# Normalizations moved to VectorE, a reordered prologue list, and the first block's query products one pair a step

## The chip, the cores and the metric

The kernel runs on one core of a Trainium2 chip. The metric is the device time of one execution in microseconds; the time before the change is the median of three runs.

## The reference

All tensors are float32 and B = 1, S = 2048, D = 512, H = 32 heads of 16, F = 1792. One key and one value head serve all 32 query heads.

```python
mod = (silu(c) @ w_mod)                       # six rows of 512: sa, ca, ga, sb, cb, gb
h = layernorm(x) * (1 + ca) + sa
q, k, v = h @ wq, h @ wk, h @ wv              # q: 32 heads; k, v: one head each
p = softmax(q k^T / 4)                        # 32 x 2048 x 2048
x = x + ga * ((p v) @ wo)
h = layernorm(x) * (1 + cb) + sb
x = x + gb * ((sigmoid(h @ w_gate) * (h @ w_up)) @ w_down)
```

## The kernel before, in words

Matrix products with weights run as three float16 products (high by high, high by low, low by high), so most activations exist as a high and a low half. The sequence is cut into four blocks b of 512 rows, and each block's 32 heads into eight units of four heads: 32 units of 16 key tiles, 512 steps in the main loop (line 969). A step computes for one unit and one tile of 128 keys four score products (`st_tile`, tile st, a PSUM bank each), four exponentials on ACT (P <- st), and the products with V and the ones column (tile c) of the step two before it. Softmax subtracts a row maximum that is found ahead: `a_product` (line 515) multiplies queries by keys into a bank sa and `a_max` (526) reduces it on DVE (mx <- sa). Four maxima are taken in each step, and `A0 = 76` of them (line 55) before step 0, so the maxima run 19 steps ahead. When a unit's 64 maxima are there, `max_end` and `max_rows` (538, 545) reduce them, transpose them on PE and write them by DMA (mh) into rows of the unit's query tile qp: the score product then has the maximum already subtracted. So a score product of a unit waits for that DMA.

The **prologue** is everything before step 0. Its order is written out by hand in the string `PLAN` (36), each token of which names a function through `stages` (861) and its arguments: `S` statistics of one x tile, `ra`, `rb`, `rc` the inverse root (DVE, POOL, DVE), `N` the normalization of a tile of 128 rows (`ln_norm`, 386), `T` four transposes on PE into a bank pt, `H`, `E`, `L` the high half (ACT), the float32 copy (ACT or DVE) and the low half (POOL or DVE) of the modulated activation, `pk`, `KB`, `KL` the key product and its evictions into kp, `pv`, `V` the value product, `q`, `QA`, `QL` a query product of 128 columns, its eviction on ACT and its low half on POOL, `pm`, `me`, `pr`, `m` the modulation, `wh`, `wl` a piece of wq into halves, `a` a maxima product, `x` the maximum on DVE, `mx` a quarter of unit 0's maxima rows, and `lw`, `lx`, `lm` loads. All engines keep this order, except for loads and some POOL work that a scheduler places. Which engine does a piece is set by tables: `NORM` (51) sends the four normalizations of block 0 to DVE and the twelve others to POOL.

A finished query group is written to DRAM (qD, line 474) and read back rearranged as qp (500): the first maxima product of a query piece waits for both DMAs. All loads and these writes are issued by SP to one DMA queue. Blocks' query groups that the prologue leaves out, ten of sixteen, run in the first block in five couples: `Couple.part` (161) issues for each term two matmuls that use one half of PE's rows each, called a pair here, 24 pairs a couple. `light` (960) hands them out to the steps, beginning at step 2: 17 steps a couple, with one or two pairs a step by the table `ats`. After the last pair both groups of the couple are evicted at once by `end` (456): ACT writes the float32 copy q32, POOL makes high and low half, SP writes qD. `defer(n, f)` (662) has f called at the start of the step n later.

After the first block the feed-forward work of the block before takes the place of `light`, and the last block's stands after the loop.

Of the kernel before, what the change touches and what calls it, by code (L numbers as in the profile page):

```python
# [10 lines left out]
AF = mybir.ActivationFunctionType  # L11
ALU = mybir.AluOpType
# [6 lines left out]
D = 512  # L19
# [10 lines left out]
SH = 4.0  # L30
SW = 16.0
# [3 lines left out]

PLAN = (
# [12 lines left out]
)  # L49

NORM = ('DDDD', 'PPPP', 'PPPP', 'PPPP')
H32 = ('ADAD', 'AAAA', 'AAAA', 'AAAA')
HLO = ('PDPD', 'PPPP', 'PPPP', 'PPPP')

A0 = 76
LAG = 2


# [9 lines left out]
QSKIP = 2  # L68
# [11 lines left out]
def adaln_mqa_glu_kernel(  # L80
# [15 lines left out]
    pool, sp = nc.gpsimd, nc.sync  # L96
# [3 lines left out]
    x = x[0]  # L100
# [30 lines left out]
    pinned, first = [True], [True]  # L131
    pe, dve, act = Ordered(nc.tensor), Ordered(nc.vector), Ordered(nc.scalar)
    pool1 = Ordered(nc.gpsimd)
# [45 lines left out]
    def t32(name, shape=(P, 512)):  # L179
        return wp.tile(list(shape), F32, tag="f32", name=name, bufs=18)  # L180
# [176 lines left out]
    def xs(b):  # L357
        return [xall[:, 4 * b + t, :] for t in range(4)]
# [26 lines left out]

    def ln_norm(b, t):
        mv, ve, rs, nw = lns[b]
        eng = dve if NORM[b][t] == 'D' else pool1
        eng.tensor_scalar(xs(b)[t], xs(b)[t], mv[:, t, 0:1], rs[:, t:t + 1], op0=ALU.subtract, op1=ALU.mult)

    def ln1_tr(b, k):
        pts[b, k] = pt = bank("pt")
# [21 lines left out]
    def passes(ah, al, bh, bl):  # L414
        return ((ah, bh), (ah, bl), (al, bh))
# [34 lines left out]
    def q_group(b, o):  # L450
        def term(n, rs):
            k, i = divmod(n, 3)
            w_, h_ = passes(wqh[k], wql[k], h1[b][0][k], h1[b][1][k])[i]
            return w_[rs, o * P:(o + 1) * P], h_[rs]

        def end(pq, second):
            qdone.add((b, o))
            q2 = wp.tile([P, 2, 512], F16, tag="q2", name="q2", bufs=2)
            q32 = t32("q32")
            act.activation(q32, pq, AF.Identity, scale=1.0 / (SH * SW))  # L460
            if first:
                act.activation(q2[:, 0], pq, AF.Identity, scale=1.0 / (SH * SW))
                q2s[b, o] = q2, q32
                return
            pool.tensor_scalar(q2[:, 0], q32, 1.0, 0.0, op0=ALU.mult, op1=ALU.add)
            q_low(b, o, q2, q32)

        return Group("q", 12, "pq", term, end)

    q2s = {}  # L470

    def q_low(b, o, q2, q32):
        (pool1 if first else pool).tensor_tensor(q2[:, 1], q32, q2[:, 0], op=ALU.subtract)
        sp.dma_start(qD[:, o * P:(o + 1) * P, b * QB:(b + 1) * QB].rearrange("h p q -> p h q"), q2)
# [63 lines left out]
    def max_end(i, t0, t1):  # L538
        nt = t1 - t0
        n = 4 * nt  # L540
        m16 = wp.tile([P, n], F32, tag="m16", name="m16", bufs=4)
        dve.tensor_reduce(m16.rearrange("p (h t) -> p h t", t=nt), mxs[i][:, :, t0:t1, :], axis=AX.X, op=ALU.max)
        return lambda: max_rows(i, t0, t1, m16)
# [118 lines left out]
    def defer(n, f_):  # L662
        waits.append((now[0] + n, f_))
# [35 lines left out]
    class Transposes:  # L699
        stage, n = "tr", 4  # L700
# [145 lines left out]
    def q_part(b, o, k):  # L846
        if k == 0:
            groups[b, o] = q_group(b, o)
        g = groups[b, o]
        if k == 0:  # L850
            g.open()
        for n in range(3 * k, 3 * k + 3):
            pe.matmul(g.bank, *g.term(n, slice(0, P)), start=(n == 0), stop=(n == g.n - 1))

    def q_end(b, o):
# [3 lines left out]
    blanks.append(blank(pool1))  # L859

    stages = {"S": ln_stats, "ra": ln_eps, "rb": ln_pow, "rc": ln_newton, "N": ln_norm, "T": ln1_tr, "H": ln1_high,
              "E": ln1_full, "L": ln1_low, "pk": k_product, "KB": k_high, "KL": k_end, "pv": v_product, "V": v_end,
              "wh": wq_high, "wl": wq_low, "q": q_part, "QA": q_end, "QL": lambda b, o: q_low(b, o, *q2s.pop((b, o))),
# [3 lines left out]
    for tok in PLAN.split():  # L867
        name = tok.rstrip("0123456789")
        stages[name](*[int(z) for z in tok[len(name):]])
    assert not held and apos == A0  # L870
    first.clear()
# [18 lines left out]
    nw, wdone = len(wjobs), 0  # L890
    qleft = [(b, o) for b in range(NB) for o in range(4) if (b, o) not in qdone]
    early = [Couple(q_group(*z), q_group(*y)) for z, y in zip(qleft[::2], qleft[1::2])]
    main, spare = [], []
    run = []
# [63 lines left out]


    def light(s):  # L960
        c_, n = divmod(s - QSKIP, 17)
        if s >= QSKIP and c_ < len(early):
            ats = [0, *(12 * (k + 1) // 9 for k in range(9)), *(12 + 12 * (k + 1) // 8 for k in range(8))]
            early[c_].part(ats[n], ats[n + 1])

    vq = []
    before = None
# [1 line left out]
    for i, (b, u) in enumerate(units):  # L969
# [4 lines left out]
        for kb in range(NKB):  # L974
            s = i * NKB + kb
# [5 lines left out]
            rows = [max_end(*z) for z in late]  # L981
            an = A0 + 4 * s

# [6 lines left out]
            if before == "run":  # L990
                piece()
            elif b == 0:
                light(s)
# [78 lines left out]
```

## Time and profile before

| | |
|---|---|
| median of 3 runs (1729.25 to 1729.74) | 1729.47 us |
| the profiled execution | 1729.32 us |
| its span | 1727.5 us |
| mean granted TensorE clock | 0.994 |
| PE busy | 1685.0 us (98%) |
| DVE busy | 1422.0 us (82%) |
| ACT busy | 1236.0 us (72%) |
| POOL busy | 635.2 us (37%) |
| first score matmul of step 0 | at 108.7 us |

Busy times overlap; matmuls are pipelined and their ends are modelled. In the answers, a row of instructions gives its start, its length, the engine, the line, what it writes and reads (out<-in), a count, and in brackets the idle time of its engine before it and what ended that. A row of waits gives the sum, the number and the longest. Nearly all prologue and loop instructions have line 129, that of the helper that keeps them in order, so the tiles' names tell them apart. PEclk is the clock granted to TensorE as a share of full speed. A row of the chain of waits gives start, length and what the chain ran through.

### The profile page before, as it was taken

Reading aid. Unit: us, or ns where it says so; the run is one execution under the profiler, and the core shown is the slowest. Engines: PE = TensorE matmul, PEld = TensorE weight load, DVE = VectorE, ACT = ScalarE, POOL = GpSimd, SP = SyncE. Lnnn points to the kernel's source line nnn. Section 1 sums busy time; section 2 is a strip of 40 time slices with the busy share of each in tenths; the row PEclk is TensorE's granted clock in tenths of the full one; section 3 lists DMA queues with packets and bytes.
Section 4 is the critical chain, followed back from the end, with each engine's and each line's share of the span. In section 5 each row is a group of like instructions: output and inputs, shape, how many; then the busy total and the mean of one; then the engine's idle time right before and its main releaser. Section 6 shows DMA issues by size and latency. Waiting matters only on the chain.

```text
span 1727.5 us, 34861 instructions
## 1 busy us (share of the span) xinstructions
PE 1685.0 (98%) x13971; PEld 571.6 (33%) x13971; DVE 1422.0 (82%) x2359; ACT 1236.0 (72%) x2253; POOL 635.2 (37%) x732
## 2 busy tenths in 40 slices
PE   5899999999999999999999999999999999999998
PEld 2323333322323333333333333333333333323443
DVE  7789999999998898988898988898898888941311
ACT  4358888888878777777778777777778777774100
POOL 6642444444254231332154232233254141231533
PEclk9899999999999999999999999999999999999999
DMA  8022232330101010111011110011101110111211
GB/s 285 1 89 66 77 101 89 94 112 29 39 24 45 29 51 11 39 45 36 25 41 32 41 48 15 26 48 50 33 25 49 32 54 5 30 50 56 76 59 49
DMA packets 66282, 90.88 MB, mean 53 GB/s; under 512 B 14800, under 2 KB 41424, under 8 KB 66120
## 3 DMA queue, kind: packets, MB, share of 16 engines
q1 hardware_dynamic: 66120, 88.66, 16.1%
q8 instruction: 109, 1.79, 0.4%
q14 instruction: 53, 0.43, 0.1%
HBM read 67.68 MB, written 16.22 MB: 49 GB/s over the span
## 4 chain that ended last, share of the span: by engine, by line
PE 89%; DVE 4%; POOL 3%; ACT 2%; DMA 1%; issue 1%; SPq 0%; POOLq 0%; DVEq 0%; ACTq 0%
PE c L129 29%; PE st L129 22%; PE pgu L129 12%; PE sa L129 9%; PE pd L129 5%; PE pgu L153 4%; PE pq L129 2%; PE pd L153 2%; DVE mx L129 2%; PE po L129 2%; ACT P L129 2%; POOL xall L129 1%; DMA xall<-in_A_x_dram 1%; PE pt L129 1%; PE po L153 1%
## 5 line engine op out<-in xcount | busy, mean ns | idle before, releaser
L129 DVE TENSOR_REDUCE mx<-sa 128x1 f32<-128x512 f32 x2048 | 1289.3, 683 | 126.3 <-PE sa L129 120.5
L129 ACT ACTIVATE P<-st 128x512 f32<-128x512 f32 x2048 | 1137.9, 596 | 274.5 <-PE sa L129 240.7
L129 PE MATMUL st<-qp,kp 64*128 64x512 f16 x2048 | 747.0, 379 | 8.9 <-ACT P L129 4.6
L129 PE MATMUL sa<-kp,qp 64*128 64x512 f16 x2048 | 747.8, 383 | 3.4 <-DVE mh L129 1.5
L129 PE MATMUL c<-P,V 128*32 128x512 f32 (+1 forms) x5296 | 577.1, 508 | 0.7 <-ACT cs L129 0.4
L129 PEld LDWEIGHTS <-kp 64*128 64x128 f16 x2048 | 174.1, 94 | 497.3 <-issue 409.3
L129 PEld LDWEIGHTS <-qp 64*128 64x128 f16 x2048 | 186.7, 93 | 175.9 <-issue 93.1
L129 PE MATMUL pgu<-h2h,gw 64*128 64x512 f16 x1344 | 242.6, 376 | 0.0
L129 PEld LDWEIGHTS c<-P,V 128*32 128x32 f32 x5296 | 104.4, 108 | 189.1 <-issue 179.8
L791 POOL TENSOR_SCALAR th<-th 128x512 f32<-128x512 f32 x42 | 25.9, 617 | 334.8 <-ACT th L129 334.8
L129 PE MATMUL pgu<-h2l,gw 64*128 64x512 f16 x672 | 132.5, 376 | 0.0
L129 PEld LDWEIGHTS <-gw 64*128 64x128 f16 x2016 | 99.6, 94 | 80.6 <-issue 2.9
L492 POOL MEMSET qp<- 32x2048 f16 x28 | 50.3, 1798 | 48.6 <-PE st L129 36.9
L153 PE MATMUL pgu<-h2h,gw 128*128 128x512 f16 x224 | 67.0, 379 | 1.2 <-POOL h2h L304 1.2
L797 POOL TENSOR_TENSOR gl<-th,gh 128x512 f16<-128x512 f32 x56 | 64.8, 1157 | 4.7
L785 ACT ACTIVATE th<-pgu 128x512 f32<-128x512 f32 x14 | 8.4, 597 | 79.3 <-PE pgu L153 79.3
L794 DVE SCALAR_TENSOR_TENSOR th<-th,pgu 128x512 f32<-128x512 f32 x14 | 9.6, 688 | 66.0 <-PE pgu L153 51.9
L273 POOL TENSOR_SCALAR wst<-wst 128x512 f32<-128x512 f32 x46 | 28.4, 618 | 90.9 <-DMA wst<-in_B_w_down_dram 35.4
L555 POOL TENSOR_SCALAR mh<-m 16x128 f16<-16x128 f32 x31 | 8.9, 288 | 139.0 <-ACT m L129 138.6
L814 POOL TENSOR_TENSOR ot<-ot,gb 128x512 f32<-128x512 f32 x10 | 12.7, 1270 | 128.6 <-ACT ot L129 128.6
L129 DVE COPY u<-pgu 128x512 f32<-128x512 f32 x42 | 28.5, 679 | 35.6 <-PE st L129 19.8
L654 POOL TENSOR_TENSOR raw<-raw,rb 128x512 f32<-128x512 f32 x15 | 19.1, 1272 | 102.4 <-DMA rb<-lD 76.8
(158 smaller groups left out, 1367.4 us busy)
## 6 DMA issues: line engine op xcount, KB each, us to landing
gw<-wD SPq DMA_DIRECT2D x56, 512.0 KB
wD<-gw SPq DMA_DIRECT2D x14, 512.0 KB
wm<-in_w_mod_dram SPq DMA_DIRECT2D x6, 1024.0 KB
qp<-qD SPq DMA_DIRECT2D x96, 64.0 KB
qD<-q SPq DMA_DIRECT2D x16, 256.0 KB
raw<-cs SPq DMA_DIRECT2D x128, 32.0 KB
xr<-in_A_x_dram SPq DMA_DIRECT2D x16, 256.0 KB
out_dram<-ot SPq DMA_DIRECT2D x16, 256.0 KB
```

Of the source, the lines that this page charges most:

```text
L129: return (lambda *a, **k: keep(f_(*a, **k))) if pinned else f_
L153: pe.matmul(self.bank, l_, r_, start=(n == 0), stop=(n == self.n - 1))
L273: pool.tensor_scalar(w_, w_, SW, 0.0, op0=ALU.mult, op1=ALU.add)
L492: eng.memset(qp[j:j + 32], 0.0)
L555: pool.tensor_scalar(mh[:, 0], m32, 1.0, 0.0, op0=ALU.mult, op1=ALU.add)
L654: keep(pool.tensor_tensor(raw, raw, rb, op=ALU.mult))
L785: act.activation(th, p_, AF.Tanh, scale=0.5 / (SH * SW))
L791: pool.tensor_scalar(th, th, 1.0, 1.0, op0=ALU.add, op1=ALU.mult)
L794: dve.scalar_tensor_tensor(th, th, 1.0, p_, op0=ALU.add, op1=ALU.mult)
L797: pool.tensor_tensor(lo, th, hi, op=ALU.subtract)
L814: pool.tensor_tensor(ot, ot, mods[5], op=ALU.mult)
```

## The change

Five things change.

1. `NORM` goes, and `ln_norm` always uses DVE: twelve pieces leave POOL.
2. `PLAN` has a new order. The four parts of the first query product come in a row, the second, third and fourth piece of wq are split later, the first maxima product stands ahead of block 1's key product, modulations 4, 3, 2 and 5 stand behind the four key products, and seven maxima products stand behind the last query product.
3. `A0` becomes 80: four more maxima before step 0, and every unit's maxima rows a step earlier.
4. `light` gives each couple one pair a step for 24 steps, and every 25th step none: the couples end at steps 25, 50, 75, 100 and 125 instead of 18, 35, 52, 69 and 86.
5. The second group of a couple is evicted one step later than the first.

```diff
-    'S10 pr0 wh0 S11 S12 wl0 T01 m0 S13 H00 T02 E01 E00 T03 ra1 H01 S20 L00 H02 E03 E02 L01 rb1 q000 H03 S21 pk00 '
...
+    'S10 wh0 S11 pr0 S12 wl0 T01 S13 T02 m0 E01 H00 T03 ra1 E00 S20 rb1 H01 E03 H02 S21 L00 E02 L01 q000 H03 rc1 '
...
-NORM = ('DDDD', 'PPPP', 'PPPP', 'PPPP')
...
-A0 = 76
+A0 = 80
...
-        eng = dve if NORM[b][t] == 'D' else pool1
-        eng.tensor_scalar(xs(b)[t], xs(b)[t], mv[:, t, 0:1], rs[:, t:t + 1], op0=ALU.subtract, op1=ALU.mult)
+        dve.tensor_scalar(xs(b)[t], xs(b)[t], mv[:, t, 0:1], rs[:, t:t + 1], op0=ALU.subtract, op1=ALU.mult)
...
             q32 = t32("q32")
+            if second:
+                defer(1, lambda: q_evict(b, o, q2, q32, pq))
+                return
+            if not first:
+                q_evict(b, o, q2, q32, pq)
+                return
             act.activation(q32, pq, AF.Identity, scale=1.0 / (SH * SW))
-            if first:
-                act.activation(q2[:, 0], pq, AF.Identity, scale=1.0 / (SH * SW))
-                q2s[b, o] = q2, q32
-                return
-            pool.tensor_scalar(q2[:, 0], q32, 1.0, 0.0, op0=ALU.mult, op1=ALU.add)
-            q_low(b, o, q2, q32)
+            act.activation(q2[:, 0], pq, AF.Identity, scale=1.0 / (SH * SW))
+            q2s[b, o] = q2, q32
...
+    def q_evict(b, o, q2, q32, pq):
+        act.activation(q32, pq, AF.Identity, scale=1.0 / (SH * SW))
+        pool.tensor_scalar(q2[:, 0], q32, 1.0, 0.0, op0=ALU.mult, op1=ALU.add)
+        q_low(b, o, q2, q32)
...
     def light(s):
-        c_, n = divmod(s - QSKIP, 17)
-        if s >= QSKIP and c_ < len(early):
-            ats = [0, *(12 * (k + 1) // 9 for k in range(9)), *(12 + 12 * (k + 1) // 8 for k in range(8))]
-            early[c_].part(ats[n], ats[n + 1])
+        c_, n = divmod(s - QSKIP, 25)
+        if s >= QSKIP and c_ < len(early) and n < 24:
+            early[c_].part(n, n + 1)
```

What stands on POOL in the prologue, before: rs are the pow rows of a block, xall the normalizations, q the first query's low half, h1l a low half of the activation.

```order
L129 TENSOR_TENSOR h1l_268<-h_272,h1h_267 128x512
L129 TENSOR_SCALAR xall<-xall,mv,rs 128x512 x3
L129 TENSOR_TENSOR rs<-ve,mhalf 128x4
L129 TENSOR_SCALAR xall<-xall,mv,rs 128x512
L129 TENSOR_TENSOR q_334<-q_335,q_334 128x512
L129 TENSOR_SCALAR xall<-xall,mv,rs 128x512
```

And in the changed kernel from the first low half on.

```order
L128 TENSOR_TENSOR h1l_246<-h_254,h1h_245 128x512
L128 TENSOR_TENSOR h1l_270<-h_276,h1h_269 128x512
L128 TENSOR_TENSOR q_308<-q_309,q_308 128x512
L128 TENSOR_TENSOR rs<-ve,mhalf 128x4
L128 TENSOR_TENSOR wdl<-wqs,wdh 128x4x128
L128 TENSOR_TENSOR h1l_368<-h_377,h1h_367 128x512
```

The first query's low half had four normalizations and a pow row ahead of it behind the last low half of block 0; now it follows that low half.

What stands on DVE at that time in the changed kernel, from the first kp eviction to the first run of maxima: nw and rs the rest of the inverse root, mx a maximum.

```order
L128 SCALAR_TENSOR_TENSOR kp<-pk,kh 128x512
L128 TENSOR_TENSOR nw<-rs 128x4
L128 SCALAR_TENSOR_TENSOR nw<-nw,ve 128x4
L128 SCALAR_TENSOR_TENSOR rs<-nw,rs 128x4
L128 TENSOR_SCALAR xall<-xall,mv,rs 128x512 x4
L128 BN_STATS st<-xall 128x6
L128 BN_AGGR mv<-st 128x2
L128 TENSOR_SCALAR ve<-mv 128x4
L128 TENSOR_REDUCE mx<-sa 128x1
L128 TENSOR_TENSOR nw<-rs 128x4
```

The normalizations of block 2 stand ahead of the first maximum; the inverse root of block 3 and its four normalizations stand behind it and so wait for the first maxima product.

On PE in the first block, a step of the kernel before with two pairs: wdl and wdh are the two halves of wq, and each pair is two matmuls on 64 rows.

```order
L129 LDWEIGHTS wdl
L129 MATMUL pq<-h1h_421,wdl 128x512
L129 LDWEIGHTS wdl
L129 MATMUL pq<-h1h_421,wdl 128x512
L129 LDWEIGHTS wdh
L129 MATMUL pq<-h1h_437,wdh 128x512
L129 LDWEIGHTS wdh
L129 MATMUL pq<-h1h_437,wdh 128x512
```

The same pairs in the changed kernel, where scores (st), maxima products (sa) and products with V (c) of a whole step stand between them.

```order
L128 MATMUL pq<-h1h_367,wdl 128x512
L128 LDWEIGHTS kp
L128 MATMUL st<-qp,kp 128x512
L128 LDWEIGHTS qp
L128 MATMUL sa<-kp,qp 128x512
L128 MATMUL c<-P_1265,V 32x256 x2
L128 MATMUL c<-P_1287,V 32x256 x2
```

Each pair now has a step of its own.

20 rows, old and new, of the table PLAN are left out of this document.

## The prediction

> **What bounds the kernel now.** I read the busy times by stage first: the end of the prologue in three windows, then the first block's 128 steps (109.8 to 441.1 us) and the second block.
>
> ```profile
> span 1727.5 us, 34861 instructions
> ```
>
> ```profile
> core 0: us, PE busy (x) PEld busy (x) DVE busy (x) ACT busy (x) POOL busy (x), PEclk, DMA share, GB/s
> 26.00:41.20 15.20, 8.79 (x83) 5.32 (x81) 9.06 (x19) 8.60 (x14) 15.19 (x11) 0.78 0.76 272
> 41.20:61.20 20.00, 14.49 (x56) 6.80 (x56) 9.46 (x17) 7.68 (x11) 20.00 (x13) 0.74 0.01 3
> 61.20:108.80 47.60, 46.02 (x339) 16.36 (x339) 42.78 (x81) 13.11 (x21) 16.57 (x14) 1.00 0.10 32
> 109.80:441.10 331.30, 324.39 (x3290) 101.12 (x3289) 319.13 (x523) 291.01 (x538) 148.12 (x185) 0.99 0.26 81
> 441.10:814.80 373.70, 372.49 (x3146) 121.48 (x3145) 338.81 (x554) 294.43 (x540) 123.88 (x146) 1.00 0.12 36
> ```
>
> POOL is full from 26 to 61 us, PE from 61 to 108.8, PE and DVE nearly together in the first block (98% and 96%), PE alone later. So the change can act in the first three rows and in the fourth.
>
> The full POOL is the normalization. The answer on the tile xall gives both prices:
>
> ```profile
> L129 POOL TENSOR_SCALAR xall<-xall,mv,rs x12: 2067/2077/2449, 24.6 to 55.2; 128x512 f32<-128x512 f32 x12
> ...
> L129 DVE TENSOR_SCALAR xall<-xall,mv,rs x4: 539/540/547, 13.8 to 15.2; 128x512 f32<-128x512 f32 x4
> ```
>
> Twelve pieces at 2.08 us, 24.9 us of POOL, against 0.54 on DVE (6.5 us for twelve). DVE has the room: in 26 to 61.2 it works 18.5 of 35.2 us, and its waits name the late maxima products.
>
> ```profile
> DVE mx L129 <- PE sa L129: 9.4, 6, 3.0
> ```
>
> **The prologue.** With the normalizations on DVE, what is late next is the first maxima product: it needs the first query, through DRAM and back. SP's queue and PE show that path:
>
> ```profile
> 18.51 5.60 SPq L207 DMA_DIRECT2D wm<-in_w_mod_dram  x4
> 35.38 0.37 SPq L474 DMA_DIRECT2D qD<-q  x1
> 37.72 2.67 SPq L500 DMA_DIRECT2D qp<-qD  x6
> ```
>
> ```profile
> 42.34 0.39 PE L129 MATMUL sa<-kp,qp 64*128 64x512 f16 x2 [0.73 <-DMA qp<-qD]
> ```
>
> The changed POOL order has only pow rows and low halves ahead of the query's low half, so I expect its write to be issued near 28.5 instead of 35.4. But the four loads issued from 18.5 are still moving: 26 to 41.2 us carries 272 GB/s by 15.2 us, 4.1 MB, nearly all of it theirs, and in the trace the write has landed when the qp loads start at 37.7. Issued sooner, it stands behind the same loads in the same queue. If the queue keeps its order, the first products stay at 41.2 and 42.3 us. I take that; if the write passed the loads it would land 2.3 us after issue (35.38 to 37.72), and all could come 6.9 us sooner.
>
> So I count PE's list from the first maxima product, at 41.2, to the first step, by the chain's prices at full clock (three matmuls or a run of products in a row):
>
> ```profile
> 66.46 0.59 PE pt L129 x4
> 67.04 0.61 PE sa L129 x2
> 67.65 0.75 PE pk L129 x3
> 68.40 0.44 PE sa L129 x2
> 68.85 1.30 PE pv L129 x48
> ...
> 77.87 0.32 PE sa L129 x2
> 78.19 1.05 PE prow L129 x2
> ...
> 84.26 0.75 PE pq L129 x3
> ```
>
> From there the changed order holds 20 pq triples (15.0), 12 pk triples (9.0), 7 groups of four transposes (4.1), 4 pv (5.2), 4 prow and 4 pmod (8 at about 1.05, 8.4), 37 runs of one or two maxima products (at 0.32, 11.8), 6 longer runs (at two to four times 0.32, together 4.1) and 4 transposes of maxima rows (at 0.37, 1.5): 59.1 us. To this come 1.6 us of idle PE, as in 61.2 to 108.8 (47.6 less 46.0), and a cold start. The granted clock in 41.2 to 61.2 was 0.74 and PE idle 5.5 us: together some 10 us lost there. In the changed order PE idles before 41.2, too, but then finds work that waits for no POOL; I put 4.5 us, between 2 and 10: 41.2 + 59.1 + 1.6 + 4.5 = 106.4 instead of 108.8. (The clock reads 0.74 in one row and 1.00 in the next. The Trainium skill, TensorE: Matmul & The Clock Gate, Part 1, has the half clock end after some 3.4 us of sustained work; by it, as an estimate, the clock's part would be 1.7 us, and with 1 us of waits the list would end 1.8 us sooner, which the forecast's band holds.)
>
> Then the transition: today the second score matmul waits for the last query's eviction.
>
> ```profile
> 109.97 0.37 PE L129 MATMUL st<-qp,kp 64*128 64x512 f16 x1 [0.85 <-ACT q L129]
> ```
>
> The changed list has its last eviction before the last seven maxima products, so about 0.6 of the 0.85 goes. Step 0 comes 3.0 us earlier: **-3.0**.
>
> DVE must keep up. Its price of a maximum:
>
> ```profile
> 212.31 9.83 DVE L129 TENSOR_REDUCE mx<-sa 128x1 f32<-128x512 f32 x16
> ```
>
> That is 0.614 us each. From 41.65: 80 maxima 49.1 (four more than before, 2.5 us of it), four normalizations of the last block 2.2, three kp and the small rows about 3.5, the four rounds of maxima rows about 6: 102.5, and 3 to 4 us of waits at the start. It ends as late as PE, with nothing to spare; A0 = 80 therefore costs its 2.5 us here, and they are in the sum. What the row below shows can be added: while POOL did two low halves back to back, a 128x4 DVE instruction took 2.25 us.
>
> ```profile
> 38.45 2.25 DVE L129 TENSOR_TENSOR nw<-rs 128x4 f32<-128x4 f32 x1 [2.94 <-POOL rs L129]
> ```
>
> The Trainium skill states this as a rule that speaks against the change (GPSIMD Engine Reference, section Key points): GpSimd shares its SBUF interfaces with VectorE and contends with DVE instructions in a two-port mode or with two SBUF inputs. The row agrees. The trace has no normalization on DVE beside POOL work, since its four ran while POOL was idle; bounds are nothing and one low half (1.15 us, half of 2.27 for two) for each of the four normalizations after 41.2: 0 to +4.6 us. Those before 41.2 are free, since DVE then waits for the first product. I take nothing, for POOL is half idle then.
>
> **The first block.** A step holds four exponentials on ACT; the starts of groups of four are a step apart.
>
> ```profile
> 205.69 2.21 ACT L129 ACTIVATE P<-st 128x512 f32<-128x512 f32 x4 [0.24 <-PE sa L129]
> 208.15 2.38 ACT L129 ACTIVATE P<-st 128x512 f32<-128x512 f32 x4 [0.24 <-PE sa L129]
> 210.81 2.19 ACT L129 ACTIVATE P<-st 128x512 f32<-128x512 f32 x4 [0.29 <-PE sa L129]
> ```
>
> ```profile
> 209.08 0.38 PE L129 MATMUL pq<-h1h,wdl 64*128 64x512 f16 x2
> 209.29 0.38 PE L129 MATMUL pq<-h1h,wdh 64*128 64x512 f16 x2
> ```
>
> ```profile
> 387.63 2.24 ACT L129 ACTIVATE P<-st 128x512 f32<-128x512 f32 x4 [0.21 <-PE sa L129]
> 390.08 2.24 ACT L129 ACTIVATE P<-st 128x512 f32<-128x512 f32 x4 [0.21 <-PE sa L129]
> ```
>
> A step with one pair (205.69 to 208.15) takes 2.46; one with two pairs (at 209.08 and 209.29) 2.66; one without, late in the block, 2.45: four maxima by 0.614 are 2.46. So the first pair is hidden under DVE, the second costs 0.20. Today's table has 7 such steps in each of 5 couples, 35; two of these fall on steps that the maxima rows lengthen anyway. 33 by 0.20: **-6.6**. The steps that today hold no pair get one at nothing, under the same cover.
>
> At a couple's end ACT evicts two groups in one step and PE waits:
>
> ```profile
> 336.82 0.37 PE L129 MATMUL st<-qp,kp 64*128 64x512 f16 x1 [0.62 <-ACT P L129]
> ```
>
> Apart, each eviction still exceeds ACT's slack (2.45 less 2.2 a step). Between nothing and 0.62 comes back at each of five ends; I take 0.2: **-1.0**.
>
> The maxima rows at a unit's end:
>
> ```profile
> 141.66 2.33 ACT L129 ACTIVATE P<-st 128x512 f32<-128x512 f32 x4 [0.29 <-PE sa L129]
> ...
> 147.32 2.19 ACT L129 ACTIVATE P<-st 128x512 f32<-128x512 f32 x4 [0.29 <-PE sa L129]
> ```
>
> Two steps, one with two pairs, take 5.66 instead of 2.46 + 2.66: 0.54 more. Three units whose ends lie beyond today's couples get pairs beside them; between 0 and 0.54 each, I take half: **+0.8**. And A0 = 80 makes every unit's rows a step earlier, so this stall should go: **-0.9** (0 to -0.9).
>
> ```profile
> 401.33 0.37 PE L129 MATMUL st<-qp,kp 64*128 64x512 f16 x1 [0.94 <-DMA qp<-mh]
> ```
>
> In the later blocks PE is the bound and keeps its work; the step less with maxima at the end I count at nothing. POOL's halves and SP's writes of the early queries only move, and POOL is idle for half of the block.
>
> **Sum.** -3.0 - 6.6 - 1.0 + 0.8 - 0.9 = -10.7. The profiled execution took 1729.3 us (span 1727.5 and 1.8 around it), 0.15 below the median of the three runs. 1729.3 - 10.7 = **1718.6 us**.
>
> **The rivals.**
> 1. *The prologue gives nothing.* DVE's normalizations wait for POOL (+4.6), or PE stays cold as it does now (10 us instead of 4.5, +5.5). With either, 1723.2 to 1724.1; for it speaks the 0.74 clock, against it that PE's waits for POOL are gone. With both, about 1729: no difference that can be measured.
> 2. *The query's write passes the loads.* First products up to 6.9 us earlier: 1711.7. Against it speaks that the write landed only when the loads' bytes were through.
> 3. *Slower: pairs in an unbroken row.* Today two one-pair steps at most stand between two-pair steps, in which DVE gains 0.20 and catches up. If the one-pair steps hide a debt on PE, 120 of them pay it. From 0.09 us a step the gain is gone; at two-pair length (2.66 in all 120 steps) the pairs cost 24.0, so 1718.6 + 24.0 = 1742.6. Against it: one-pair steps at 2.46 beside each other, no longer than DVE's own 2.46.
> 4. *The change doesn't do what it says:* the late eviction still meets the next step's exponentials and gives nothing: 1719.6, inside the forecast.
>
> **How the numbers follow.** The forecast (1715 to 1722) has 0.62, rival 1 as 1722 to 1725.8 has 0.17 and its worst, within 0.2%, 0.07, rival 2 0.07, rival 3 0.07. The range takes in the forecast, most of rival 1 and rival 2: 1711.5 to 1725.5. About 0.2% (3.5 us) is what a measurement of this kernel can tell from no change. Faster 0.86, same 0.07, slower 0.07.
>
> **What would show it.** Right: POOL no longer full before 61 us; the first maxima product still near 41 us, after an idle PE; step 0 near 107; one-pair steps at 2.45 throughout the first block, which takes about 324 us. Wrong: normalizations on DVE well over 0.54 us, a clock below 1 long after 48 us, steps above 2.5 with one pair, or later blocks that change by over 1 us.

## The result, and the profile after

| | before | after |
|---|---|---|
| median of 12 runs | 1729.61 us | 1728.88 us |
| range | 1729.06 to 1730.69 | 1726.37 to 1733.87 |
| span of the profiled execution | 1727.5 us | 1729.0 us |
| first exponential of step 0 | 109.80 us | 108.85 us |
| the 128 steps of the first block | 331.3 us | 333.5 us |
| blocks 2 to 4, to the last step | 1136.5 us | 1136.7 us |

The ratio is 0.9999, with an interval of 0.9991 to 1.0008: no difference that can be measured, where I forecast 10.7 us less. The runs spread over 7.5 us, before's over 1.6.

The stages first: span, then busy time of PE, PEld, DVE, ACT and POOL, the granted clock, DMA share and GB/s in the windows that the prediction showed of before.

```profile
span 1729.0 us, 34862 instructions
```

```profile
26.00:41.20 15.20, 9.76 (x40) 4.56 (x38) 13.42 (x27) 10.36 (x17) 7.39 (x7) 0.82 0.76 271
41.20:61.20 20.00, 19.11 (x131) 8.64 (x129) 19.55 (x32) 13.09 (x19) 13.98 (x13) 0.88 0.01 2
61.20:108.80 47.60, 44.51 (x324) 15.45 (x324) 38.29 (x74) 9.79 (x17) 9.39 (x8) 0.93 0.16 50
109.80:441.10 331.30, 322.25 (x3277) 102.77 (x3276) 318.77 (x523) 285.69 (x535) 142.80 (x179) 0.98 0.24 77
```

POOL is no longer full, and PE works 19.1 us of 41.2 to 61.2 instead of 14.5. But the clock, 1.00 in before's third window, is 0.93 in this one, and 0.98 in the first block.

The normalizations cost about what I took (all sixteen, min/median/max in ns). The first query's write was issued 4.8 us sooner, but its reading back began only 0.6 us sooner, as if the write had landed only when the loads had (run 11 tests this); the first two maxima products came at 40.4 and 43.6 instead of 41.2 and 42.3:

```profile
L128 DVE TENSOR_SCALAR xall<-xall,mv,rs x16: 532/542/1385, 13.9 to 48.9; 128x512 f32<-128x512 f32 x16
```

```profile
18.56 5.54 SPq L206 DMA_DIRECT2D wm<-in_w_mod_dram  x4
30.54 0.37 SPq L479 DMA_DIRECT2D qD<-q  x1
37.09 2.67 SPq L505 DMA_DIRECT2D qp<-qD  x6
```

One-pair steps in an unbroken row stay at 2.45 us, the distance of two such rows:

```profile
307.62 2.21 ACT L128 ACTIVATE P<-st 128x512 f32<-128x512 f32 x4 [0.24 <-PE sa L128]
310.07 2.21 ACT L128 ACTIVATE P<-st 128x512 f32<-128x512 f32 x4 [0.24 <-PE sa L128]
```

Two rows further the row breaks. The next unit's first score product waits 3.74 us for its maxima rows, and then PE runs at half clock (0.58 for a product of 0.37, 1.08 for eight products with V of 0.64):

```profile
312.66 0.64 PE L128 MATMUL c<-P,V 128*32 128x256 f32 x8
317.04 0.58 PE L128 MATMUL st<-qp,kp 64*128 64x512 f16 x1 [3.74 <-DMA qp<-mh]
...
318.43 1.08 PE L128 MATMUL c<-P,V 128*32 128x256 f32 x8
```

Steps 79, 80 and 81 take 6.46, 4.41 and 3.02 us. All that each step of the first block took above 2.455 us (four maxima at 0.614), from the starts of the groups of four exponentials:

| us above 2.455 a step | before | after |
|---|---|---|
| steps 0 to 2 | 0.3 | 2.3 |
| other steps, each under 0.25 (before: 24 with two pairs, 4.6) | 5.2 | 0.2 |
| the five couples' ends | 5.0 | 2.8 |
| maxima rows, evictions of c | 5.8 | 5.7 |
| waits for maxima rows at steps 32 and 112 | 0.9 | 1.8 |
| steps 79 to 81 | in the rows above | 6.5 |
| sum | 17.1 | 19.3 |

So the pairs brought 5.0 (4.6 in the 24 steps that had two, 0.4 at two evictions of c, steps 33 and 65) and the ends 2.2, as meant, and two new losses took it: 6.5 behind step 79 and 2.0 in the first three steps. In step 0 PE now waits for DVE's maxima where it waited for the last query's eviction:

```profile
109.92 0.40 PE L128 MATMUL sa<-kp,qp 64*128 64x512 f16 x2 [0.87 <-DVE mx L128]
```

How the rows came late can be read in two queues. ACT had evicted the transposed maxima (m) at 304.65; POOL, which makes their halves (mh), came to them at 312.24 and 313.62, and SP issued their writes behind that:

```profile
304.65 0.27 ACT L128 ACTIVATE m<-sa 16x128 f32<-16x128 f32 x1
```

```profile
303.80 1.16 POOL L478 TENSOR_TENSOR q<-q,q 128x512 f16<-128x512 f32 x1
...
307.57 0.62 POOL L472 TENSOR_SCALAR q<-q 128x512 f16<-128x512 f32 x1
309.83 0.62 POOL L272 TENSOR_SCALAR wst<-wst 128x512 f32<-128x512 f32 x1 [1.65 <-DMA wst<-in_B_w_up_dram]
310.53 1.16 POOL L478 TENSOR_TENSOR q<-q,q 128x512 f16<-128x512 f32 x1
...
312.24 0.29 POOL L560 TENSOR_SCALAR mh<-m 16x128 f16<-16x128 f32 x1
312.50 1.15 POOL L274 TENSOR_TENSOR gw<-wst,gw 128x512 f16<-128x512 f32 x1
313.62 0.41 POOL L561 TENSOR_TENSOR mh<-m,mh 16x128 f16<-16x128 f32 x1
```

```profile
304.99 0.37 SPq L479 DMA_DIRECT2D qD<-q  x1
305.41 0.46 SPq L271 DMA_DIRECT2D wst<-in_B_w_up_dram  x1
311.71 0.36 SPq L479 DMA_DIRECT2D qD<-q  x1
312.55 1.38 SPq L569 DMA_DIRECT2D qp<-mh  x2
314.02 0.39 SPq L688 DMA_DIRECT2D wD<-gw  x1
314.51 1.31 SPq L569 DMA_DIRECT2D qp<-mh  x2
```

POOL and SP each keep their order. The third couple now ends at step 75, its second group is evicted at 76, and 76 is also the step of a unit's maxima rows, needed from step 80. A weight load (wst) stands on SP behind the first group's write, POOL waits for it, and the second group's halves and the rows stand behind that.

### The profile page after: what moved, and what is told of

It is laid out like the page before. It is cut to its first block, busy times and chain, and to the rows that moved or that the text cites. A ratio compares the mean times of both kernels' runs of the same rounds, so it can differ in the third digit from the quotient of the medians.

```text
span 1729.0 us, 34862 instructions
## 1 busy us (share of the span) xinstructions
PE 1689.2 (98%) x13971; PEld 574.4 (33%) x13971; DVE 1431.1 (83%) x2371; ACT 1232.7 (71%) x2253; POOL 610.7 (35%) x720
## 4 chain that ended last, share of the span: by engine, by line
PE 87%; DVE 4%; DMA 3%; POOL 2%; ACT 2%; issue 1%; SPq 1%; POOLq 0%; ACTq 0%; DVEq 0%
PE c L128 27%; PE st L128 21%; PE pgu L128 12%; PE sa L128 9%; PE pd L128 5%; PE pgu L152 4%; DVE mx L128 3%; PE pq L128 2%; PE pd L152 2%; PE po L128 2%; ACT P L128 1%; DMA wst<-in_B_w_up_dram 1%; PE pt L128 1%; DMA xall<-in_A_x_dram 1%; PE po L152 1%
## 5 line engine op out<-in xcount | busy, mean ns | idle before, releaser
L128 DVE COPY u<-pgu 128x512 f32<-128x512 f32 x42 | 28.6, 681 | 38.6 <-PE st L128 22.6
L659 POOL TENSOR_TENSOR raw<-raw,rb 128x512 f32<-128x512 f32 x15 | 19.1, 1272 | 105.4 <-DMA rb<-lD 67.4
L797 POOL TENSOR_TENSOR th<-th,u 128x512 f32<-128x512 f32 x42 | 53.3, 1270 | 3.5
```

What stands on the lines that cost most here:

```text
L128: return (lambda *a, **k: keep(f_(*a, **k))) if pinned else f_
L659: keep(pool.tensor_tensor(raw, raw, rb, op=ALU.mult))
L797: pool.tensor_tensor(th, th, u_, op=ALU.mult)
```

## The experiments

**Theory A**: the pairs and ends save some 7 us, and this meeting gives 6.5 back. **B**: the loss is in the prologue. **C**: POOL's weight halves are late wherever a couple ends. All times are medians; before's lay between 1729.7 and 1730.0 beside them.

**1. The pairs alone.** Before, with the new `light` and the late second eviction.

```diff
-        c_, n = divmod(s - QSKIP, 17)
+        c_, n = divmod(s - QSKIP, 25)
...
+            if second:
+                defer(1, lambda: q_evict(b, o, q2, q32, pq))
+                return
```

> The list, the normalizations and A0 = 76 of before, with one pair a step and the second eviction a step later. Theory A (the pairs save about 7 us, and the third couple's halves, queued on POOL and SP ahead of a unit's maxima rows at step 76, give 6.5 us of it back): the rows come at step 77 here, one step later than in the changed kernel, and are needed at step 80 all the same, so the stall is there and at least as long: 6.5 to 9 us, a time of 1728 to 1731. Theory B (the loss is in the prologue and what it leaves behind): no stall near step 80, the gain is kept, 1721 to 1723.

Measured: 1728.92 us, ratio 0.9994 (0.9985 to 1.0003). Steps 79 to 81 take 6.40, 5.10 and 3.57, 7.7 us above three times 2.455. A holds: the stall comes without the new prologue.

**2. The prologue alone.** The changed kernel with `light` and eviction of before.

```diff
-        c_, n = divmod(s - QSKIP, 25)
+        c_, n = divmod(s - QSKIP, 17)
...
-            if second:
-                defer(1, lambda: q_evict(b, o, q2, q32, pq))
-                return
```

> The list, the normalizations on DVE and A0 = 80 of the changed kernel, with the pairs and evictions of before. Theory A: the prologue's end comes 1 us earlier and steps 0 to 2 are 2 us longer, so it is worth between +0.2 and +1.5 us; the couples end at step 69 and 86, no halves lie ahead of the rows at step 76: 1729.5 to 1731. Theory B: the prologue loses what the pairs gain, some 6 us: 1735. My prediction's prologue term alone (-3.0, and -0.9 for the stall that goes): 1725.7.

Measured: 1729.72 us, 1.0004 (0.9995 to 1.0013). Steps 79 and 80 are normal, steps 0 and 2 take 3.31 and 3.87. The profile has the first exponential at 106.21, 2.6 us sooner than the changed kernel's, with the same list up to there: the prologue's length varies from execution to execution. The eleven runs fall into two groups, six from 1727.8 to 1729.7 at a mean granted clock of 0.994 to 0.996 and five from 1730.5 to 1733.8 at 0.992 or 0.993. B's 1735 is wrong: the prologue doesn't lose what the pairs gain. But it gains nothing where my prediction's terms gave 1725.7, so 4.0 us of the miss lie here.

**3. The third couple later.** The changed kernel; its evictions now follow the rows of step 76.

```diff
-        c_, n = divmod(s - QSKIP, 25)
+    STARTS = (2, 27, 54, 79, 104)
```

> The changed kernel, with only the third and the later couples begun two steps later, so that the third one's evictions come at steps 77 and 78, behind the maxima rows of step 76. Theory A: the wait of 3.7 us for the maxima rows at step 80 and the half clock after it go, 6 to 7 us less: 1722 to 1723. Rival C (the stall comes from the weight halves on POOL, which wait for a load that SP issues late behind the reciprocals' way through DRAM, wherever the couple ends): the wait stays over 3 us, 1728 to 1729.

Measured: 1725.78 us, 0.9976 (0.9967 to 0.9986). The rows' writes were issued ahead of the couple's, at 303.67, and the stall at step 80 is gone:

```profile
303.67 2.79 SPq L569 DMA_DIRECT2D qp<-mh  x4
307.11 0.37 SPq L479 DMA_DIRECT2D qD<-q  x1
```

Of the 6 to 7 us only 3 came: the wait at step 112 grew, to steps of 3.86 and 4.89. No couple ends there; POOL does weight halves (of w_down) and the attention's rows in its order, and makes mh 7 us after ACT's m:

```profile
383.79 0.27 ACT L128 ACTIVATE m<-sa 16x128 f32<-16x128 f32 x1 [0.18 <-PE sa L128]
```

```profile
388.68 2.27 POOL L274 TENSOR_TENSOR wdl<-wst,wdh 128x512 f16<-128x512 f32 x2
390.92 0.29 POOL L560 TENSOR_SCALAR mh<-m 16x128 f16<-16x128 f32 x1
```

So A is right for step 80, and C is right that any unit's rows can be caught in that queue. Why the wait at step 112 is longer here than in the changed kernel, with the same work around it, no run shows.

**4. Pairs, both groups evicted at once.** As run 1, with before's eviction; against before only `light` differs.

```diff
-        c_, n = divmod(s - QSKIP, 17)
+        c_, n = divmod(s - QSKIP, 25)
```

> As the run with the pairs alone, but both groups of a couple are evicted at once as before. Against that run five steps get an eviction more and five one less: PE waits up to 0.55 us more at each of five ends, 1 to 2.5 us in all, by the steps' lengths in the changed kernel (3.00 for the first eviction, 2.46 for the second). Theory A: both groups' halves are queued at step 75 and not 75 and 76, so the rows of step 77 meet a queue that is up to one step shorter: the stall near step 80 is 0 to 2.5 us shorter. Sum of both: within 2.5 us of that run.

Measured: 1729.18 us, 0.9996 (0.9987 to 1.0004). Near run 1, but not for the reason given: the stall at 79 to 81 lost 5.5 us (steps of 3.38, 3.35, 2.80), far more than 2.5. SP's queue shows why. In run 1 one weight load stood between the two writes, as in the changed kernel:

```profile
303.41 0.37 SPq L481 DMA_DIRECT2D qD<-q  x1
303.83 0.46 SPq L272 DMA_DIRECT2D wst<-in_B_w_up_dram  x1
310.83 0.36 SPq L481 DMA_DIRECT2D qD<-q  x1
```

Here it was issued ahead of both, and POOL did not wait for it:

```profile
300.67 0.90 SPq L272 DMA_DIRECT2D wst<-in_B_w_up_dram  x1
305.26 2.31 SPq L474 DMA_DIRECT2D qD<-q  x2
```

The five ends got longer by 0.4 each, and the fifth couple, with both groups now at step 125, stands ahead of that step's rows: steps 127 and 128 are 1.25 and 1.78 longer than in run 1, with two waits for them (sum, number and longest, from 438 to 460 us):

```profile
PE st L129 <- DMA qp<-mh: 1.6, 2, 1.2
```

The stall follows the meeting.

**5. The changed kernel, both groups at once.**

```diff
-            if second:
-                defer(1, lambda: q_evict(b, o, q2, q32, pq))
-                return
```

> The changed kernel, with both groups of a couple evicted at once as before. Theory A now reads: the stall at step 80 comes from the second group's halves and its write a step later, behind which a weight load is issued too late and POOL waits 1.7 to 2.4 us for it, ahead of the maxima rows. Then the wait of 3.7 us goes down to under 1 us and the half clock after it goes (-6), and the five couple ends get longer again by 0.43 each (+2.2, by 0.98 and 0.55 in the two runs with the pairs alone): 1724 to 1726. Rival C (the queue is late wherever the second group is evicted): 1729 to 1731.

Measured: 1728.06 us, 0.9993 (0.9982 to 1.0004). The steps moved as theory A says: 79 to 81 lost 4.0 us and the ends gained 2.1; the wait at step 32 is gone as well, and the first block is 2.8 us shorter. The median fell by 0.8, and the runs lie between 1725.2 and 1734.9. My 1724 to 1726 had counted on 6 us from the stall; a wait of 1.27 us and one of 0.70 are left at step 80, where I had expected under 1.

**6. The third couple later, and A0 = 76.** As run 3, without the last four of the seven maxima products at the list's end.

```diff
-    'q113 x a x a QA11 x a x a QL11 x a x a x a x x x '
+    'q113 x a x a QA11 x a x QL11 x x '
-A0 = 80
+A0 = 76
```

> As the run with the third couple later, but A0 = 76: the last four of the seven maxima products behind the last query product go. Theory D (seven maxima at DVE's pace leave PE idle for 2.0 of the 4 us before step 0, the granted clock falls to 0.5 and steps 0 to 2 take 2 us more; and four maxima on a full DVE cost 2.5 us): step 0 comes 2 to 2.5 us earlier and steps 0 to 2 lose 1 us at most, 3 to 4 us less, against which the maxima rows stand a step nearer to their use (0 to +1.5): 1722 to 1724. Rival (the four maxima only move: DVE has as many before the rows of each unit either way): 1725 to 1727.

Measured: 1721.00 us, 0.9949 (0.9937 to 0.9962), 4.8 less than run 3 and below my range. Steps 0 to 2 lost their 2.4 us entirely; another 2.4 came at steps 111 to 113 (1.8 above three times 2.455 instead of 4.2), where I had expected nothing or a loss. Step 0 itself did not come earlier in the profiled execution (first exponential at 107.18, 106.57 in run 3), in which the clock fell twice on the way (see run 10). The end of the prologue, columns as above, run 3 first:

```profile
104.00:108.00 4.00, 2.12 (x12) 0.64 (x10) 4.00 (x7) 1.75 (x4) 3.00 (x4) 1.00 1.02 321
108.00:112.00 4.00, 3.42 (x15) 0.92 (x12) 4.00 (x8) 3.13 (x6) 3.61 (x6) 0.61 0.38 117
112.00:116.00 4.00, 4.00 (x28) 0.83 (x26) 3.28 (x6) 2.62 (x5) 3.76 (x5) 0.54 0.00 0
```

And with A0 = 76:

```profile
104.00:108.00 4.00, 3.20 (x16) 0.87 (x15) 3.74 (x7) 1.91 (x4) 1.15 (x1) 1.00 0.80 250
108.00:112.00 4.00, 3.86 (x17) 1.28 (x15) 4.00 (x8) 4.00 (x8) 3.57 (x6) 1.00 0.89 292
112.00:116.00 4.00, 4.00 (x41) 1.09 (x38) 4.00 (x8) 2.98 (x7) 3.76 (x6) 1.00 0.02 4
```

In run 3 DVE is full, PE works 2.1 of 4 us, and the clock is 0.61 and 0.54 for the next 8. With fewer maxima at the end PE idles less and stays at full clock. The other profiles agree: all five with seven maxima at the list's end have 6.8 us of half clock at this place and lose 2.2 to 2.5 us in steps 0 to 2, and the three without half clock there and with A0 = 76 and all normalizations on DVE (runs 6, 7, 10) lose 0.0; those with 3.4 us of half clock there lose 0.3 to 1.3. The half clock is not all of it: 1.2 of the 2.4 are in step 0, in which PE waits 0.87 and 0.58 us for DVE's maxima, most of it before the clock falls.

**7. The normalizations alone.** Before, with all twelve on DVE.

```diff
-NORM = ('DDDD', 'PPPP', 'PPPP', 'PPPP')
+NORM = ('DDDD', 'DDDD', 'DDDD', 'DDDD')
```

> Before, with only the twelve normalizations moved from POOL to DVE. If they alone carry the prologue's gain (POOL is no longer full to 61 us; step 0 stood at 105.6 to 108.8 in the three kernels with the changed list, 109.8 to 110.8 in the three with the old one): step 0 near 107, steps 0 to 2 as before, 1726 to 1727.5. If the order of the list carries it, or DVE's rows beside POOL cost what they save: 1729 to 1731.

Measured: 1724.34 us, 0.9967 (0.9955 to 0.9980), and 1723.5 to 1724.5 in all runs. The first exponential is at 105.03 and steps 0 to 2 are normal; the time is below my range. So one part of the change is worth 5.5 us alone, more than I gave the whole prologue; with the new list and A0 = 80 (run 2) nothing is left of it.

**8. The maxima rows on DVE.** The changed kernel; `max_rows` takes its prologue branch throughout.

```diff
-        if not first:
+        if False:
             m32 = wp.tile([n, P], F32, tag="m32", name="m32", bufs=4)
```

> The changed kernel, with the halves of the maxima rows made by DVE from PSUM, as the prologue does it, and not by ACT and POOL. The four writes of the rows still stand behind the second query group's write on SP, which waits for POOL's low half. If POOL's queue alone held the rows, the stall at step 80 goes: -6.5, less up to 1.5 for seven rounds on DVE: 1722 to 1724. If SP's order holds them too, the writes are issued at about 311.7 instead of 312.5 to 314.5 and the wait is 1 to 2 us instead of 3.7: 1724.5 to 1727. If neither, 1729.

Measured: 1727.27 us, 0.9986 (0.9978 to 0.9995). The second reading holds, its time missed by 0.3: DVE had both halves before 303, but SP issued their writes 7 us later, behind the second group's:

```profile
302.37 0.28 DVE L128 SCALAR_TENSOR_TENSOR mh<-sa,mh 16x128 f16<-16x128 f32 x1
```

```profile
309.20 0.36 SPq L479 DMA_DIRECT2D qD<-q  x1
309.62 2.79 SPq L569 DMA_DIRECT2D qp<-mh  x4
```

The wait fell from 3.74 to 1.72 and 0.76; the wait at step 112 went altogether. Steps 79 to 81 are only 0.8 us shorter (5.7 above three times 2.455 instead of 6.5), since the clock falls to half at 312.9 for 6.8 us here, too.

**9. Normalizations and pairs.** Run 7 with run 3's couples and the late second eviction.

```diff
-NORM = ('DDDD', 'PPPP', 'PPPP', 'PPPP')
+NORM = ('DDDD', 'DDDD', 'DDDD', 'DDDD')
...
+    STARTS = (2, 27, 54, 79, 104)
```

> Before's list and A0 = 76, with the normalizations on DVE, one pair a step, the second eviction a step later, and the third and later couples begun two steps later. If the parts add: the normalizations alone gave 1724.3, and the first block's steps took 16.5 us above 128 times 2.455 there against 11.6 in the run with A0 = 76 and the third couple later: 1724.3 - 4.9 = 1719.4, between 1718.5 and 1720.5, with step 0 near 105. If the list is needed for it, or a stall of over 2 us comes up at another unit: 1722 or more.

Measured: 1718.33 us, 0.9932 (0.9920 to 0.9944): the parts add (0.2 below my range), and the new list is not needed. Run 6 differs from this run in the list alone and is 2.7 us slower, so the new order looks like a loss; the runs of the two overlap (1719.4 to 1722.2 there, 1717.4 to 1720.7 here), so its size is rough.

**10. Thin matmuls set apart.** As run 6; the value products (16 columns) and the modulation's products and sums in the list's last third alternate with query products.

```diff
-... pv1 x KL3 a x a pv2 V1 x x a a pm4 V2 x x a a me4 pm3 x x a a me3 pr4 ...
+... pv1 x KL3 a x a q010 V1 x x a a pv2 q011 x x a a V2 pm4 x x a a q012 me4 ...
```

> As the run with A0 = 76 and the third couple later (1721.0), with the thin matmuls of the list's end (value products of 16 columns, modulation products and sums) set apart by the wide query products that stood behind them; the same work in all. Theory E (in half of the profiles of the changed list the granted clock fell to 0.5 twice for 3.4 us, each time behind 3.4 us in which PE was busy with thin matmuls alone): the clock is 1.00 from 50 to 104 us, and 1.5 to 3.4 us go: 1717.5 to 1719.5. Rival F (the fall has nothing to do with the kind of matmul): the clock falls as before, 1720.5 to 1721.5; or PE and DVE wait more for the new order and it is slower.

Measured: 1721.02 us, 0.9950 (0.9937 to 0.9964): as run 6. The profiled execution did have the clock at 1.00 from 50 to 104 us and was the fastest of five (1718.6), but the others reached 1725.2. E is not confirmed. What it was made for, in the changed kernel:

```profile
63.00:66.40 3.40, 3.40 (x98) 2.56 (x98) 3.40 (x8) 0.02 (x1) 1.32 (x1) 1.00 0.00 0
66.40:69.80 3.40, 3.40 (x18) 0.30 (x10) 3.18 (x6) 0.60 (x1) 0.00 (x0) 0.50 0.02 5
69.80:73.20 3.40, 3.40 (x30) 2.38 (x30) 2.45 (x6) 0.60 (x1) 0.00 (x0) 0.99 0.00 0
73.20:76.60 3.40, 3.40 (x17) 0.30 (x9) 2.19 (x4) 0.60 (x1) 0.00 (x0) 0.51 0.00 0
```

PE is busy throughout by the profile, in the first row mostly with value products (83 of 91 matmuls begun there) and in the third mostly with modulation sums of one column (16 of 26), and after each the clock is halved for 3.4 us. Run 3, with the same list:

```profile
66.40:69.80 3.40, 3.40 (x30) 0.79 (x26) 3.40 (x8) 0.92 (x2) 0.00 (x0) 1.00 0.02 5
73.20:76.60 3.40, 3.40 (x20) 1.04 (x17) 3.01 (x6) 1.73 (x3) 0.00 (x0) 1.00 0.01 2
```

**11. Loads behind the query.** As run 9; three modulation loads stand behind the first query's write and its reading back, and SP keeps that order.

```diff
-    'lw0 lx2 lx3 lw1 lw2 lw3 lm4 lm3 lm2 lm5 pm1 ...
+    'lw0 lx2 lx3 lw1 lw2 lw3 lm4 pm1 ...
-... L12 me4 a a a L13 ...
+... L12 me4 a lm3 lm2 lm5 a a L13 ...
```

> As the run with the normalizations on DVE and the pairs, but three of the four modulation loads are issued behind the first query's write and its reading back. My prediction's reason for a first maxima product that stays near 41 us was that the write stands behind the loads in the queue: then it comes 3 to 5 us earlier here (35.5 to 38), and 0 to 4 us of that reach step 0. If something else sets it (the rearranged reading, POOL), it stays at 40 to 41 and the time is that of the other run within 1 us.

Measured: 1717.09 us, 0.9925 (0.9913 to 0.9937); the runs overlap run 9's, so its 1.2 us are not certain. The write landed 2.3 us after its issue instead of 6.6 to 7.1:

```profile
30.33 0.37 SPq L481 DMA_DIRECT2D qD<-q  x1
32.66 2.69 SPq L509 DMA_DIRECT2D qp<-qD  x6
```

The first maxima product came at 38.6, only 2.3 us sooner than in run 9, short of the 3 to 5 that I expected: now DVE is late, with rows of 128x4 that take 1.1 us beside POOL.

**12. The same, with the maxima rows on DVE** (the edit of run 8).

> As the run with the loads behind (1717.1), and the halves of the maxima rows made by DVE from PSUM. In the changed kernel that took away the wait at step 112 (3.41 us to under 2.7) and left the steps with maxima rows at 3.00, so DVE pays nothing that can be seen. Here the steps 111 to 113 took 4.5 us above three times 2.455: 1 to 4 us less if POOL's queue holds those rows, 1713 to 1716; if SP's order holds their writes, the same within 1 us.

Measured: **1713.87 us**, 0.9904 (0.9888 to 0.9921), 1713.4 to 1713.95 in all four runs. No score product of the first block waits for its maxima rows any more, and steps 111 to 113 went from 4.2 us above three times 2.455 to 0.3. It beats both kernels, by 15.8 and 15.0 us.

## Why the prediction was wrong, step by step

**Where the miss lies.** The pairs and ends were to bring 6.8 us (-6.6 - 1.0 + 0.8); alone they brought 0.8 (run 1). The prologue with A0 = 80 was to bring 3.9 (-3.0 - 0.9); alone it brought nothing (run 2).

**The step that failed** is the one on the moved evictions and the maxima rows behind them. The evictions were put at nothing, on the ground that "POOL's halves and SP's writes of the early queries only move, and POOL is idle for half of the block", and the rows were to gain: "A0 = 80 makes every unit's rows a step earlier, so this stall should go: **-0.9**". That stall stayed (step 112 at 3.41 us, 3.35 before), and steps 32 and 79 to 81 came out 7.4 us longer (0.9 and 6.5, with the half clock behind the stall). Idle on average was no cover: the halves moved to step 76, ahead of a unit's rows in two queues that keep their order, one of which waits for a load. I had compared POOL's busy time and not what stands ahead of the rows where they now fall. For steps 79 to 81 runs 1, 3, 4, 5 and 8 show the cause; for the 0.9 at step 32 no run does.

**The prologue, -3.0**: the way to step 0 came out in size, its worth did not. The first score product stands at 105.4 to 108.5 (mean 106.9) in the five profiles with this list and A0 = 80, and at 108.7 to 109.8 (mean 109.3) in the three with the old list and normalizations: -2.4, as I had it. The first exponential, for which PE no longer waits on the last eviction, even comes 3.1 sooner (means 107.3 and 110.3). But step 0 then waits for DVE instead. What I missed is that seven maxima at DVE's pace behind the last query product leave PE idle; I had counted them only as DVE time. That wait and the half clock after it cost 2.0 in steps 0 to 2 (run 6), so of the 3.1 about -1.1 is left. The right size was partly luck. The new list had no term of its own and by runs 6 and 9 costs some 2.7; the normalizations alone bring 5.5 (run 7), and four more maxima cost 2.4 in steps 0 to 2 (run 6). That makes -0.4, against nothing in run 2.

**Normalizations at 0.54**: right for ten of twelve; two, beside a low half on POOL, took 1.38. My nothing for the contention was short by 1.7 us on them; POOL, which I called half idle there, was busy for 14.0 of the 20 us from 41.2. Six DVE rows of 128x4 beside POOL's low halves took 0.97 to 1.12 instead of 0.16, 5.4 us too long in all, but before, six of them beside POOL's low halves and normalizations had lost 4.3.

**The write behind the loads** kept its place: right, as run 11 shows, where it had landed 4.9 us sooner than in run 9. Rival 2 is out.

**Two-pair steps, -6.6**: they brought 5.0 (24 steps of 0.19, and 0.4 at two evictions of c), not 33 times 0.20. **Couples' ends, -1.0**: 2.2; the second group's eviction costs nothing in a step of its own, the first 0.55. Rival 4 is out. **Maxima rows, +0.8**: 1.0 (steps 93, 109 and 125 were 0.65 above 2.455 in all; with a pair beside them such rows take 0.54 each). **Rival 3** named a slower time through PE's debt in one-pair steps; they stayed at 2.45.

**The terms together**, prologue, pairs, ends, rows and stalls, -1.1 - 5.0 - 2.2 + 1.0 + 7.4, give +0.1; the stall also swallows an eviction of c at step 81 and a unit's rows at 76, 0.7 in all, which makes -0.6, near the measured -0.7.

**Rival 1** had the clock in it, though mostly at another place: from 41 to 61 us PE was cold for less time than before (0.88 against 0.74), but its clock fell later (0.93 from 61.2 to 108.8, 1.00 before), which the prediction had named as a sign of being wrong. By these rows PE lost, as an estimate, 9.7 us from 41.2 to 108.8 (idle 0.9 and 3.1, clock 0.12 of 20.0 and 0.07 of 47.6), where I had put 4.5 + 1.6.

**What stays open** is why the clock falls at 66 and 73 us in some executions of the changed list and not in others (in the profiles of runs 5 and 6 it did, of 2, 3 and 8 not). The twelve runs of the changed kernel go from 1726.4 us at a mean clock of 0.994 to 1733.9 at 0.990, so most of its spread is time at half clock; but setting the thin products apart did not move the median.

## What to carry to other kernels

Before moving work to another step, look up in each in-order queue that it uses (here POOL and SP) what will then stand behind it and when that is needed; an engine idle half of the time hides nothing from an instruction queued behind a wait. Try the parts of a change apart: here one table entry alone gained 5.5 us, and together with the new list nothing. A list that ends in work for one engine leaves the other idle, and here TensorE then paid for it at half clock as well.

## What the runs showed of the hardware

An idle of 1.9 us in 4 us of PE was followed by some 7 us at half clock (run 3: 0.61 and 0.54), and the stall of 3.74 us by half-clock products to 322 us. The Trainium skill, TensorE: Matmul & The Clock Gate, Part 1 (What's actually happening) has the clock set by activity in a free-running window of about 3.4 us, after which the halves of 3.4 us at 66.4 and 73.2, and their coming in some executions only, agree. It names idleness as what throttles; here both falls followed 3.4 us in which the profile, which models the ends of matmuls, has PE busy 3.40 of 3.40, mostly with matmuls of 16 columns or one. That such matmuls are the cause is not shown: run 10 set them apart and the median stayed.

A write issued behind four loads, 4 MB, took 6.6 to 7.1 us to land (the changed kernel, run 9), and 2.3 us when three of the four were issued behind it (run 11). The Trainium skill, DMA: Bandwidth & Descriptors (HWDGE ordering) has each DMA engine take descriptors in the order of the ring; by that, the trace agrees.

In proportion DVE's smallest rows lose most beside POOL's low halves: six rows of 128x4 took 0.97 to 1.12 us in the changed kernel instead of 0.16, two normalizations of 128x512 1.38 instead of 0.54.
